# Banded attention and two MLPs: queries divided by the slope, and a part of VectorE's work given to GpSimd

## The chip, the cores and the metric

One core of one Trainium2 chip runs the whole program. The metric is the time of one execution on the device in microseconds (us). Less is better. TensorE is PE here, VectorE is DVE, ScalarE is ACT, GpSimd is POOL, and SyncE is SP, which issues the DMAs.

## The reference

```python
def _attn_ref(q, k, v, n_global, n_local):     # B 2, H 8, S 768, D 64; n_global 8, n_local 96
    scores = scale * np.matmul(q, k.transpose(0, 1, 3, 2))
    is_global = pos[None, :] < n_global
    is_local = (rel >= 0) & (rel < n_local)
    dist = np.where(is_global & ~is_local, n_local, np.abs(rel))
    slopes = 2.0 ** (-8.0 * (np.arange(H) + 1) / H)
    scores = np.where(is_global | is_local, scores - slopes[:, None, None] * dist, -1e9)
    a = np.exp(scores - np.max(scores, axis=-1, keepdims=True))
    a = a / (np.sum(a, axis=-1, keepdims=True) + 1e-09)
    return np.matmul(a, v)
def _moe_ref(x, w_in, w_out):                  # 1536 tokens, 512 -> 2048 -> 512
    h = np.maximum(x @ w_in, 0.0)
    return h * h @ w_out
def _moe2_ref(x, w_gate, w_val, w_out, rms_g): # 512 -> 1536 -> 512
    xn = x / np.sqrt(np.mean(x * x, axis=-1, keepdims=True) + 1e-06) * rms_g
    g = xn @ w_gate
    return (g / (1.0 + np.exp(-g)) * (xn @ w_val)) @ w_out
```

The output is `_moe2_ref(_moe_ref(attention))`, in float32.

## The kernel before, in words

**Three stages.** The attention comes first, in 16 slices (4 chunks of 384 tokens by 4 pairs of heads) of 3 tiles of 128 queries, so 48 tiles. The first MLP follows in 4 groups of hidden blocks; each group passes over the 4 token chunks, and the first passes of group 0 are mixed into the attention. Then the rows are normalised, and the second MLP is done with 7 products in place of 8 (sums of blocks are multiplied, lines 507 to 545).

**Products in three parts.** A float32 matrix is kept as a high part (fp32r, cast by ACT in L305) and a low part (the rest, a subtraction in L306). `mm3` issues three matmuls per product: high by high (L315), high by low (L316), low by high (L317). `xh`/`xl` are the split inputs of an MLP, `h` the hidden activations (L415 squares them), `M`, `ar` and `H` are slots for split weights, `b` is a bank of PSUM (the accumulators of the matmuls), `y` the sums of the first MLP (L446) and the output of the second (L588).

**Weights.** The weights come as eight-byte words and are turned into float32 by `expand()`: a DMA into `wraw` (L341), one ACT instruction (L344) and four of DVE on `wbits` (L345, L347, L349, L352). `block()` then splits the result. The low part (L306) is made on DVE for groups 0 and 1 and on POOL for the others.

**An attention tile.** The keys and queries of a slice arrive in `raw`. `prep` makes their high part `kqh` (L762 on ACT once, L764 on POOL) and low part `kql` (L766, DVE). PE multiplies them (L795, the "QK" product) into `ps`. L802 (DVE) adds the bias of the head and takes the row's extreme in one pass; the bias is a tile of its own for each head, made by POOL in L779 (`bw` for 256 keys, `bo` for 128). L806 (ACT) takes the exponential and the sum, L810 (DVE) adds 1e-9, L813 (DVE) takes the reciprocal, L815 (POOL) multiplies. PE transposes (`tb`, L822), ACT copies (`pt`, L824), PE multiplies by the values (`av`, L831).

**The norm.** `norm_sum` squares on ACT (into `nq`), adds three times on DVE (L464, `ns`), lets PE sum over the partitions with a matrix of ones (L466), takes the root on ACT (L469) and three reciprocals on DVE (L472). `norm(p)` then makes for each half of the tokens, twice, four scaled blocks (`fin`, L493, DVE) and four differences T1 to T4 (`diff`, L498, POOL), and splits all eight: the B blocks' low parts on DVE, the T blocks' on POOL (L306 with `ar<-nq` or `xl<-nq`).

**What sets the order.** Every instruction is put into a `Plan` with an engine, an assumed duration, the tiles it reads and writes, and for some a due time. `solve()` takes for each engine the ready instruction with the earliest due time, starts it when the assumed end of its predecessors plus a margin of their engine (`LAT`) is reached, and each engine's instructions are then written out in that order of starts. So a changed duration or margin can move any instruction, and on the chip an engine keeps its order whatever happens. Where PE has nothing planned before 30 us, `solve` puts in fillers, matmuls on a tile of zeros whose result nobody reads (L1085). At the end of the program a flag (L912 to L917) is loaded into a register of every engine (`values_load`, L1089) and a branch tests it (L1090); the branch holds a general attention that these inputs don't need.

## Time and profile before

| | before |
|---|---|
| runs, us | 705.15, 701.94, 702.2; median 702.2 |
| the profiled execution: its own time | 700.68 us |
| its span (first to last instruction) | 698.9 us |
| busy | PE 94%, DVE 71%, ACT 54%, POOL 36% |
| PE's clock over the span, of full speed | 0.997 |

The span is what the trace covers; 1.8 us of the execution's own time lie around it. "Busy" is an average over stages with different limits, so the rows below are cut by stretch: the attention (to about 165 us), the middle of the first MLP (to 330), its last group with the norms (330 to 470), and the second MLP (470 to the end).

### The profile page before, as it was taken

To read this page: it belongs to the slowest core of one execution; us is meant where nothing else is said; L and a number is where in the kernel's file an instruction comes from. 1 tells how busy PE (TensorE), PEld (TensorE's weight loads), DVE (VectorE), ACT (ScalarE), POOL (GpSimd) and SP (SyncE) were. 2 spreads that over 40 slices of the span, in tenths; PEclk is the share of its full clock that TensorE was granted. 3 is DMA by queue.
4 is the path that set the end of the run, shared out by engine and by line. 5 is a ranking of instruction groups with operands and counts; after the bars stand their busy time and mean duration, and the time that the engine had idled before them with its cause. 6 is when DMAs were issued, how large, how long until landed. Compare 5 with 4: busy or idle time off the path is not lost.

```text
span 698.9 us, 10714 instructions
## 1 busy us (share of the span) xinstructions
PE 657.8 (94%) x3876; PEld 591.8 (85%) x3876; DVE 495.2 (71%) x1025; ACT 374.4 (54%) x834; POOL 248.5 (36%) x298
## 2 busy tenths in 40 slices
PE   6999999998999999989899788999999999999996
PEld 6766777778989999989898677899898898997994
DVE  4899975556787722258898997976967868768434
ACT  2778786778755433356765666654344344343320
POOL 4855655430022000022518567635234323332000
PEclk9999999999999999999999999999999999999999
DMA  4554643201333300003220000121220311210022
GB/s 141 181 164 143 196 133 97 75 24 59 101 112 122 121 1 0 1 31 118 94 61 1 30 32 30 61 92 59 78 75 30 115 53 44 91 61 0 2 76 110
DMA packets 18159, 52.69 MB, mean 75 GB/s; under 512 B 2608, under 2 KB 3888, under 8 KB 18096
## 3 DMA queue, kind: packets, MB, share of 16 engines
q1 hardware_dynamic: 18096, 51.92, 22.6%
q8 instruction: 32, 0.52, 0.3%
q14 instruction: 31, 0.25, 0.1%
HBM read 48.76 MB, written 3.15 MB: 74 GB/s over the span
## 4 chain that ended last, share of the span: by engine, by line
PE 31%; DVE 16%; ACT 2%; issue 2%; POOL 2%; POOLq 0%; DVEq 0%
PE b L315 10%; PE b L317 10%; PE b L316 10%; DVE wbits L349 3%; DVE h L306 2%; DVE ra L564 1%; DVE wbits L345 1%; DVE wbits L347 1%; DVE ns L472 1%; DVE xl L306 1%; DVE h L415 1%; DVE wbits L352 1%; DVE y L588 1%; DVE nq L493 1%; POOL nq L498 1%
## 5 line engine op out<-in xcount | busy, mean ns | idle before, releaser
L306 POOL TENSOR_TENSOR M<-wbits,M 128x512 fp32r<-128x512 f32 x60 | 82.0, 1371 | 254.3 <-ACT M L305 168.9
L315 PE MATMUL b<-xh,M 128*128 128x384 f32 x384 | 133.4, 347 | 1.2 <-DVE xl L306 1.2
L316 PE MATMUL b<-xl,M 128*128 128x384 f32 x384 | 129.1, 336 | 0.5 <-DVE xl L306 0.5
L317 PE MATMUL b<-xh,M 128*128 128x384 f32 x384 | 129.0, 336 | 0.0
L815 POOL TENSOR_SCALAR p<-p,rs 128x256 f32<-128x256 f32 (+1 forms) x96 | 59.2, 628 | 54.6 <-DVE rs L813 29.5
L315 PEld LDWEIGHTS b<-xh,M 128*128 128x128 f32 x384 | 72.2, 188 | 6.9 <-issue 1.9
L316 PEld LDWEIGHTS b<-xl,M 128*128 128x128 f32 x384 | 72.4, 189 | 2.7 <-DVE xl L306 1.0
L415 DVE TENSOR_TENSOR h<-ra,h 128x384 fp32r<-128x384 f32 x64 | 42.3, 666 | 42.9 <-ACT ra L414 42.7
L317 PEld LDWEIGHTS b<-xh,M 128*128 128x128 f32 x384 | 72.4, 188 | 0.1
L305 ACT CAST M<-wbits 128x512 fp32r<-128x512 f32 x68 | 41.9, 617 | 49.5 <-DVE wbits L352 27.1
L349 DVE SCALAR_TENSOR_TENSOR wbits<-wraw,wbits 128x512 int32<-128x512 int32 x68 | 62.3, 917 | 1.8
L588 DVE TENSOR_TENSOR y<-b,y 128x512 f32<-128x512 f32 x60 | 40.9, 688 | 28.2 <-PE b L317 27.9
L317 PE MATMUL b<-M,h 128*128 128x512 f32 x144 | 56.9, 395 | 3.9 <-DVE h L306 3.9
L315 PE MATMUL b<-M,h 128*128 128x512 f32 x144 | 56.9, 395 | 3.1 <-DVE y L588 3.0
L806 ACT ACTIVATE p<-p,mn 128x256 f32<-128x256 f32 (+1 forms) x96 | 46.5, 487 | 22.0 <-DVE mn L802 21.3
L412 ACT ACTIVATE ra<-b 128x384 f32<-128x384 f32 x64 | 31.1, 486 | 50.6 <-PE b L317 50.6
L316 PE MATMUL b<-M,h 128*128 128x512 f32 x144 | 56.8, 394 | 0.0
L344 ACT ACTIVATE wbits<-wraw 128x512 f32<-128x512 f32 x68 | 45.4, 668 | 18.1 <-DMA wraw<-in_w_gate_dram 7.5
L345 DVE TENSOR_SCALAR wbits<-wbits 128x512 f32<-128x512 f32 x68 | 39.3, 578 | 20.5 <-ACT wbits L344 18.6
L305 ACT CAST h<-ra 128x384 fp32r<-128x384 f32 x48 | 24.6, 514 | 46.4 <-DVE ra L564 45.7
L352 DVE SCALAR_TENSOR_TENSOR wbits<-wraw,wbits 128x512 int32<-128x512 int32 x68 | 48.2, 709 | 1.2
L316 PE MATMUL b<-h,ar 128*128 128x384 f32 x128 | 43.5, 339 | 3.4 <-DVE h L415 3.4
(125 smaller groups left out, 1613.9 us busy)
## 6 DMA issues: line engine op xcount, KB each, us to landing
wraw<-in_w_out_dram SPq DMA_DIRECT2D x28, 512.0 KB, 3.5
wraw<-in_w_in_dram SPq DMA_DIRECT2D x16, 512.0 KB, 3.5
wraw<-in_w_gate_dram SPq DMA_DIRECT2D x12, 512.0 KB, 3.4
wraw<-in_w_val_dram SPq DMA_DIRECT2D x12, 512.0 KB, 3.4
raw<-in_kq_dram SPq DMA_DIRECT2D x8, 480.0 KB, 4.0
v<-in_vab_dram SPq DMA_DIRECT2D x8, 384.0 KB, 3.1
out_dram<-y SPq DMA_DIRECT2D x12, 256.0 KB, 2.0
raw<-in_kq_dram SPq DMA_DIRECT2D x7, 416.0 KB, 3.3
```

Of the source, the lines that this page charges most:

```text
L305: self.op("ACT", ACT(n), lambda: nc.scalar.copy(dst()[0], src()), rs, [(x, "hi") for x in ws])
L306: self.op(eng, t(n), lambda: e.tensor_tensor(out=dst()[1], in0=src(), in1=f32(dst()[0]), op=ALU.subtract), rs + [(x, "hi") for x in ws], [ ...
L315: nc.tensor.matmul(ps, lhsT=wh, rhs=ah, start=first, stop=False, skip_group_check=True)
L316: nc.tensor.matmul(ps, lhsT=wh, rhs=al, start=False, stop=False, skip_group_check=True)
L317: nc.tensor.matmul(ps, lhsT=wl, rhs=ah, start=False, stop=last, skip_group_check=True)
L345: self.plan.add("DVE", FAST(512), lambda: v.tensor_scalar(out=tl(bits), in0=tl(bits), scalar1=LEAST, scalar2=MOST, op0=ALU.max, op1=ALU.mi ...
L349: self.plan.add("DVE", DVE(512), lambda: v.scalar_tensor_tensor(out=bi(), in0=tl(raw)[:, :, 0], scalar=29, in1=bi(), op0=ALU.logical_shift ...
L352: self.plan.add("DVE", DVE(512), lambda: v.scalar_tensor_tensor(out=bi(), in0=tl(raw)[:, :, 1], scalar=-(1 << 30), in1=bi(), op0=ALU.bitwi ...
L415: self.op("DVE", DVE(CH), lambda: nc.vector.tensor_tensor(out=get()[1], in0=t(), in1=f32(get()[0]), op=ALU.subtract), rt + hi, lo)
L588: self.op("DVE", DVE(DM), lambda tok=tok, ps=ps: nc.vector.tensor_tensor(out=self.o(tok), in0=ps(), in1=self.o(tok), op=ALU.add), [("b", b ...
L806: self.op("ACT", 0.33 + w / 1200, lambda j=j: nc.scalar.activation(tl(f"p{m}")[:, j, :w], tl(f"p{m}")[:, j, :w], AF.Exp, bias=tl(f"mn{m}") ...
L815: self.op("POOL", 0.2 + w / 800, lambda j=j: nc.gpsimd.tensor_scalar(out=tl(f"p{m}")[:, j, :w], in0=tl(f"p{m}")[:, j, :w], scalar1=rs()[:, ...
```

## The change

1. The queries are divided by the head's slope while they are split (high part on POOL, low part on DVE, both with a column of `inv`, eight POOL memsets). The distance tiles `rel` and `t0` then serve all heads, with the slope in the scale of the DVE pass; the sixteen bias tiles of L779 go.
2. The 1e-9 is added on POOL (L812) instead of DVE (L810).
3. The low parts of the weights of groups 0 and 1 are made on POOL, those of the T blocks of the norm on DVE.
4. The flag is computed and loaded inside the plan, with due times of 100 and 130 us; before, the load stood behind everything on every engine but SP.
5. The planner's margins are larger, its DMA cost is another, the ones-matmul gets a slack of 1 us, and fillers begin at 5 us and are 0.3 us apart.
6. The weights of group 3 go into other slots and are queued earlier (`in` behind group 1, `out` and the first gate weights behind group 2).

Numbers of lines in the changed kernel are mostly one higher (L306 is L307, L345 is L346); in the attention L795 is L797, L802 is L804, L813 is L815, L815 is L817.

```diff
-    def add(self, eng, dur, emit, r=(), w=(), due=None, mode=None, lat=None):
+    def add(self, eng, dur, emit, r=(), w=(), due=None, mode=None, lat=None, slack=0.0):
...
-                x = max(free[e], 1.0)
-                while x + 0.2 < t:
+                x = max(free[e] + 0.1, 5.0)
+                while x + 0.3 < t:
                     self.fill.append(x)
-                    x += 0.18
+                    x += 0.3
...
-                    heappush(wait[q.eng], (q.ready, q.n, q))
+                    heappush(wait[q.eng], (q.ready + q.slack, q.n, q))
...
-LAT = {"PE": 0.27, "DVE": 0.17, "ACT": 0.22, "POOL": 0.22, "SP": 2.2, "END": 0.0}
+LAT = {"PE": 0.35, "DVE": 0.28, "ACT": 0.33, "POOL": 0.4, "SP": 2.6, "END": 0.0}
...
-DMA = lambda kb: 0.3 + kb / 200.0
+DMA = lambda kb: max(0.45, kb / 320.0)
...
-            due=self.clock, mode="full")
+            due=self.clock, mode="full", slack=1.0)
...
-                self.split(tmp[n], get, CH, res[n], r, "POOL" if n[0] == "T" else "DVE")
+                self.split(tmp[n], get, CH, res[n], r, "DVE")
...
+                elif kind == "in":
+                    slot = self.ar_slot(G1 + f) if f else self.m_slot(8)
                 else:
-                    slot = self.m_slot((8, 0, 1, 2)[f]) if kind == "in" else self.ar_slot(G1 + 1 + f)
-                self.block((kind, g * G1 + f), slot, "DVE" if g < 2 else "POOL")
+                    slot = self.m_slot(f - 1) if f else self.ar_slot(8)
+                self.block((kind, g * G1 + f), slot, "POOL")
...
+            if g == 1:
+                self.weights("in", 3)
             if g == 2:
-                self.weights("in", 3)
                 self.weights("out", 3)
-        for kind in ("gate", "val", "out2"):
+                self.weights("gate", 0)
+        for kind in ("val", "out2"):
...
-            if s == 0 and n == 0:
+            if n == 1:
+                self.op("POOL", POOL1(w), lambda raw=raw, hi=hi: nc.gpsimd.tensor_scalar(
+                    out=hi(), in0=raw(), scalar1=inv(), scalar2=1.0, op0=ALU.mult, op1=ALU.mult), rr + ["inv"], rh)
+                self.op("DVE", DVE(w), lambda raw=raw, hi=hi, lo=lo: nc.vector.scalar_tensor_tensor(
+                    out=lo(), in0=raw(), scalar=inv(), in1=f32(hi()), op0=ALU.mult, op1=ALU.subtract), rr + rh + ["inv"], rl)
+                continue
+            if s == 0:
...
-            name = self.bias(2 * hp + j, i)
+            name = "rel" if i else "t0"
...
-        self.op("DVE", 0.2, lambda: nc.vector.tensor_scalar(
-            out=rs(), in0=tl(f"sm{m}"), scalar1=1.0e-9, scalar2=None, op0=ALU.add),
+        self.op("POOL", 0.15, lambda: nc.gpsimd.tensor_scalar(
+            out=rs(), in0=tl(f"sm{m}"), scalar1=1.0e-9, scalar2=1.0, op0=ALU.add, op1=ALU.mult),
...
+        plan.add("DVE", 1.0, lambda: said.update(flag=covered(nc, const, nl, ng)), ["nl"], ["flag"], due=100.0)
+        plan.add("SP", 1.0, lambda: said.update(value=nc.values_load(said["flag"][0:1, 0:1], min_val=0, max_val=1)),
+                 ["flag"], (), due=130.0)
...
-    flag = covered(nc, const, nl, ng)
-    value = nc.values_load(flag[0:1, 0:1], min_val=0, max_val=1)
-    with tc.If(value < 1):
+    with tc.If(said["value"] < 1):
```

**POOL, from the first bias to the first products of probabilities** (`p` holds probabilities, `rs` the reciprocal of their sums, `sm` the sums), before:

```order
L779 TENSOR_SCALAR bo_136<-t_130 128x128
L779 TENSOR_SCALAR bo_142<-t_130 128x128
L764 TENSOR_SCALAR kqh_125<-raw_85 128x384
L779 TENSOR_SCALAR bw_153<-rel 128x256
L779 TENSOR_SCALAR bw_159<-rel 128x256
L779 TENSOR_SCALAR bo_170<-t_130 128x128
L779 TENSOR_SCALAR bo_173<-t_130 128x128
L779 TENSOR_SCALAR bw_181<-rel 128x256
L764 TENSOR_SCALAR kqh_188<-raw_116 128x448
L764 TENSOR_SCALAR kqh_188<-raw_116 128x384
L779 TENSOR_SCALAR bw_208<-rel 128x256
L815 TENSOR_SCALAR p_177<-p_177,rs_205 128x128 x2
```

and now:

```order
L767 TENSOR_SCALAR kqh_129<-raw_83,inv 128x384
L775 TENSOR_SCALAR kqh_145<-raw_113 128x448
L767 TENSOR_SCALAR kqh_145<-raw_113,inv 128x384
L812 TENSOR_SCALAR rs_191<-sm_174 128x2
L817 TENSOR_SCALAR p_168<-p_168,rs_191 128x128 x2
L775 TENSOR_SCALAR kqh_129<-raw_83 128x448
L1079 TENSOR_LOAD flag
L812 TENSOR_SCALAR rs_238<-sm_200 128x2
L767 TENSOR_SCALAR kqh_129<-raw_83,inv 128x384
L817 TENSOR_SCALAR p_187<-p_187,rs_238 128x256 x2
```

The bias tiles are gone from between the splits, the adds and the load of the flag stand in the queue.

**PE, from its first instruction to the second QK product of the attention**, before and now:

```order
L1085 MATMUL b_93<-h_91 128x384 x30
L795 MATMUL ps_162<-kqh_125 128x128
L795 MATMUL ps_164<-kqh_125 128x128
L795 MATMUL ps_162<-kql_139,kqh_125 128x128
L795 MATMUL ps_164<-kql_139,kqh_125 128x128
L795 MATMUL ps_162<-kqh_125,kql_139 128x128
L795 MATMUL ps_164<-kqh_125,kql_139 128x128
L1085 MATMUL b_93<-h_91 128x384 x5
```

```order
L1096 MATMUL b_143<-h_81 128x384 x2
L797 MATMUL ps_151<-kqh_129 128x128
L797 MATMUL ps_153<-kqh_129 128x128
L797 MATMUL ps_151<-kql_138,kqh_129 128x128
L797 MATMUL ps_153<-kql_138,kqh_129 128x128
L797 MATMUL ps_151<-kqh_129,kql_138 128x128
L797 MATMUL ps_153<-kqh_129,kql_138 128x128
L1096 MATMUL b_143<-h_81 128x384 x5
```

Two fillers stand ahead of the first QK product in place of thirty; in all, 27 are left of 76.

**DVE, at the norm sum of the first chunk** (group 3 of the first MLP), before and now:

```order
L464 TENSOR_TENSOR ns_3266<-ns_3266,nq_3274 128x384
L446 TENSOR_TENSOR y_106<-b_620,y_106 128x384
L446 TENSOR_TENSOR y_106<-b_93,y_106 128x384
L345 TENSOR_SCALAR wbits_531<-wbits_531 128x512
L347 TENSOR_SCALAR wbits_531<-wbits_531 128x512
L464 TENSOR_TENSOR ns_3266<-ns_3266,nq_3306 128x384
L464 TENSOR_TENSOR ns_3266<-ns_3266,nq_3310 128x384
L349 SCALAR_TENSOR_TENSOR wbits_531<-wraw_254,wbits_531 128x512
```

```order
L465 TENSOR_TENSOR ns_3253<-ns_3253,nq_3267 128x384
L447 TENSOR_TENSOR y_121<-b_521,y_121 128x384
L447 TENSOR_TENSOR y_121<-b_143,y_121 128x384
L465 TENSOR_TENSOR ns_3253<-ns_3253,nq_3288 128x384
L465 TENSOR_TENSOR ns_3253<-ns_3253,nq_3293 128x384
L346 TENSOR_SCALAR wbits_260<-wbits_260 128x512
L348 TENSOR_SCALAR wbits_260<-wbits_260 128x512
L350 SCALAR_TENSOR_TENSOR wbits_260<-wraw_140,wbits_260 128x512
```

The two weight instructions have moved behind the norm's adds. Over the last five chunk passes of the first MLP, DVE has 24 of these weight instructions where it had 40; the other 16 now stand in the passes before 330 us.

## Rows read from the trace of the kernel before

**Rows 1.** Windows of the whole program: us; busy time (instructions) by engine; PE clock; DMA.
```profile
8.00:40.00 32.00, 30.53 (x240) 23.37 (x238) 24.22 (x93) 20.33 (x66) 25.81 (x49) 1.00 0.49 159
40.00:82.00 42.00, 40.44 (x305) 30.88 (x306) 40.23 (x119) 33.82 (x88) 21.34 (x29) 1.00 0.50 166
82.00:330.00 248.00, 241.96 (x1559) 221.69 (x1558) 146.94 (x359) 147.10 (x343) 56.60 (x82) 1.00 0.23 73
330.00:470.00 140.00, 125.29 (x662) 116.12 (x661) 122.60 (x173) 86.82 (x171) 80.63 (x69) 0.99 0.16 53
470.00:699.00 229.00, 217.02 (x1111) 197.18 (x1110) 157.25 (x266) 84.53 (x168) 62.55 (x59) 1.00 0.18 61
```

**Rows 2.** PE's waits in 330 to 470: engine line <- releaser: us, times, longest.
```profile
PE b L466 <- DVE ns L464: 5.4, 3, 2.2
PE b L317 <- DVE h L306: 3.9, 2, 3.3
...
PE b L316 <- DVE h L415: 1.2, 2, 0.7
```

**Rows 3.** Timeline of PE, 0 to 13: start, busy, instruction, idle before it.
```profile
5.47 6.88 PE L1085 MATMUL b<-h 128*128 128x384 f32 x30 [5.47 <-DVE h L1066]
12.28 0.33 PE L795 MATMUL ps<-kqh 64*128 64x128 f32 x2
```

**Rows 4.** Timeline of POOL, 0 to 13.
```profile
7.88 1.16 POOL L779 TENSOR_SCALAR bo<-t 128x128 f32<-128x128 f32 x2 [5.74 <-DVE t L869]
9.01 0.51 POOL L764 TENSOR_SCALAR kqh<-raw 128x384 fp32r<-128x384 f32 x1
```

**Rows 5.** Timeline of DVE, 0 to 13.
```profile
7.29 0.15 DVE L917 CAST flag<-cb 128x1 int32<-128x1 f32 x1
...
9.55 0.56 DVE L766 TENSOR_TENSOR kql<-raw,kqh 128x384 fp32r<-128x384 f32 x1 [1.03 <-POOL kqh L764]
```

**Rows 6.** Timeline of SP's DMA issues, 0 to 16.
```profile
10.18 0.33 SPq L737 DMA_DIRECT2D raw<-in_kq_dram  x1
```

**Rows 7.** DVE's groups by form, 8 to 82: busy us, mean ns, idle before.
```profile
L306 DVE TENSOR_TENSOR M<-wbits,M 128x512 fp32r<-128x512 f32 x8 | 6.5, 809 | 0.0
...
L810 DVE TENSOR_SCALAR rs<-sm 128x2 f32<-128x2 f32 x22 | 4.7, 215 | 0.2 <-ACT p L806 0.2
```

**Rows 8.** POOL's groups by form, 8 to 82.
```profile
L779 POOL TENSOR_SCALAR bw<-rel 128x256 f32<-128x256 f32 x8 | 3.6, 450 | 0.3
...
L779 POOL TENSOR_SCALAR bo<-t 128x128 f32<-128x128 f32 x8 | 2.8, 359 | 5.9 <-DVE t L869 5.7
```

**Rows 9.** POOL's groups by form, 330 to 470.
```profile
L306 POOL TENSOR_TENSOR M<-wbits,M 128x512 fp32r<-128x512 f32 x17 | 24.2, 1431 | 21.3 <-ACT M L305 16.4 <-issue 4.9
...
L306 POOL TENSOR_TENSOR ar<-nq,ar 128x384 fp32r<-128x384 f32 x12 | 15.4, 1294 | 0.9 <-ACT ar L305 0.9
...
L306 POOL TENSOR_TENSOR xl<-nq,xh 128x384 fp32r<-128x384 f32 x4 | 5.4, 1361 | 0.0
```

**Rows 10.** DVE's groups by form, 330 to 470.
```profile
L349 DVE SCALAR_TENSOR_TENSOR wbits<-wraw,wbits 128x512 int32<-128x512 int32 x14 | 15.0, 1073 | 0.3
...
L306 DVE TENSOR_TENSOR xl<-nq,xh 128x384 fp32r<-128x384 f32 x12 | 11.6, 964 | 1.9 <-ACT xh L305 1.8
```

**Rows 11.** Timeline of DVE around the first norm sum.
```profile
338.34 1.44 DVE L345 TENSOR_SCALAR wbits<-wbits 128x512 f32<-128x512 f32 x1 [1.64 <-POOL M L306]
339.81 0.43 DVE L347 TENSOR_SCALAR wbits<-wbits 128x512 int32<-128x512 int32 x1
340.16 1.22 DVE L464 TENSOR_TENSOR ns<-ns,nq 128x384 f32<-128x384 f32 x2
341.29 0.68 DVE L349 SCALAR_TENSOR_TENSOR wbits<-wraw,wbits 128x512 int32<-128x512 int32 x1
```

**Rows 12.** Windows around PE's longest stop in the second norm.
```profile
418.00:421.00 3.00, 0.00 (x0) 0.00 (x0) 3.00 (x3) 0.92 (x2) 3.00 (x4) 1.00 0.00 0
421.00:423.00 2.00, 1.37 (x4) 0.85 (x5) 2.00 (x4) 0.10 (x1) 0.98 (x1) 0.63 0.00 0
```

More of the change, by code (lines that the diff above doesn't have):

```diff
@@ L56 @@
 class Op:
-    __slots__ = ("eng", "dur", "lat", "emit", "deps", "succ", "due", "mode", "start", "end", "left", "ready", "n")
+    __slots__ = ("slack", "eng", "dur", "lat", "emit", "deps", "succ", "due", "mode", "start", "end", "left", "ready", "n")
 class Plan:
@@ L635, in rest @@
         self.weights("out", 2)
+        self.used = {}
+        self.ring = deque(self.m_slot(n) for n in (3, 4, 5, 6, 7, 8, 0, 1, 2))
         for g in range(1, N1):
@@ L711, in __init__ @@
                 tl.define(f"{k}{n}", pool, [P, 2], F32)
-        for h in range(H):
-            tl.define(f"bw{h}", pool, [P, W], F32)
-            tl.define(f"bo{h}", pool, [P, P], F32)
+        tl.define("inv", pool, [P, HP], F32)
         tl.define("rel", pool, [P, W], F32)
@@ L856, in iotas, with inverse @@
             nc.gpsimd.iota(kidx(), pattern=[[1, P]], base=0, channel_multiplier=0, allow_small_or_imprecise_dtypes=True)
-        self.op("POOL", 1.5, iotas, (), y1)
+        def inverse():
+            for h in range(H):
+                nc.gpsimd.memset(tl("inv")[h % 2 * D : h % 2 * D + D, h // 2 : h // 2 + 1], 1.0 / slope8(h))
+        self.op("POOL", 1.0, iotas, (), y1)
+        self.op("POOL", 0.8, inverse, (), ["inv"])
         ts = lambda o, i, s1, s2, p0, p1: lambda: v.tensor_scalar(
@@ L1065 @@
         att = Attention(nc, plan, tl, ap, psa, mlp, kq, vab, ident, nl, ng)
-        plan.add("DVE", 0.5, lambda: nc.vector.memset(f32(tl(f"h{HB - 1}")), 0.0), (), [("h", HB - 1)])
+        plan.add("DVE", 0.5, lambda: nc.vector.memset(f32(tl(f"h{HB - 1}")), 0.0), (), [("h", HB - 1)], due=4.5)
         plan.add("POOL", 1.5, lambda: (make_identity(nc, ident), nc.gpsimd.memset(ones, 1.0), nc.gpsimd.memset(epst, 1.0e-6)),
```

22 lines of the change are left out of this document (9 added, 13 removed).

## Prediction

> **What bounds the kernel now.** I first cut the span into stretches and read each engine's busy time [rows 1]. PE works nearly without a break from 82 to 330 us (241.96 of 248), so nothing that other engines save there can shorten it much. Three stretches are different. From 8 to 40 and from 40 to 82 PE lacks 1.47 and 1.56 us, 3.0 together, while DVE is full in the second of them (40.23 of 42) and POOL is the fullest of the helpers in the first (25.81 of 32). From 330 to 470, PE lacks 14.7 us (140 less 125.29), the largest loss of the program. In the second MLP it lacks 12.0 of 229.
>
> Then I read PE's waits in 330 to 470 [rows 2]: 5.4 us for the norm's adds on DVE (three waits, the longest 2.2), 3.9 us in two waits for a low part of `h` that DVE makes, 1.2 us for squared activations. Last I read the start. PE's first real product is issued at 12.28, right behind thirty fillers that took 6.88 us from 5.47 [rows 3], although its last input was there at 9.55 + 0.56 = 10.11 [rows 5]. That input was late too: DVE waited 1.03 us for POOL, which had made two bias tiles of 1.16 us first [rows 4, 5].
>
> **The change, part by part.** The sum is made against the profiled execution, 700.68 us, which is 1.5 below the median of the runs, 702.2.
>
> *Attention, to 163 us.* DVE loses its adds (22 by 215 ns, 4.7 us, in 8 to 82) and the weights' low parts (8, 6.5 us) [rows 7]: 11.2 us less. POOL loses the bias tiles (3.6 + 2.8 = 6.4 us [rows 8]) and gains 8 low parts of 1.43 us [rows 9], 11.4 us, and 22 small adds. No row shows such an add on POOL: below, DVE's 0.215 for the same is the nearest; above, POOL's 0.359 for 128 columns [rows 8]. I take the lower, as the operand has two columns: 4.7 us (up to 7.9). So POOL goes from 47.2 to 56.9 of 74 us [rows 1]. It doesn't become full on average.
>
> POOL's work slows DVE. Where it is busy 58% of the time, L349 takes 1073 ns in the mean [rows 10] against 0.68 us by itself [rows 11], 0.39 more; a single L345 took 1.44 where its like, L347, took 0.43 [rows 11], 1.0 more. I take between 0.39 and 1.0 for each low part that comes to POOL, 3.1 to 8 us, and 4 for the sum, nearer to the mean of fourteen than to the single case. The Trainium skill states the harder rule (SBUF — State Buffer, section "Who interferes with whom"): a DVE instruction with two SBUF inputs, or in a two-port mode, and a GpSimd instruction that reads SBUF exclude each other, and the loser is blocked for the whole instruction. By that rule the eight would cost up to 11.4 us, DVE would have 2.9 us more work than before with the load below, and the sum would end at 697.1; the rows agree that there is a loss, and their 0.39 is far from the whole 1.43.
>
> The flag's load now stands in the middle of five queues. Between the flag's cast, done at 7.44, and SP's next DMA at 10.18 lay 2.74 us [rows 5, 6]; but that DMA stood right behind the split that ended at 10.11 [rows 5], which may be what held it. So a load costs an engine 0 to 2.74. I take 2.7 once, on DVE, where it sits between the two L802 of one tile. DVE is left with 11.2 - 4 - 2.7 = 4.5 us less work. At the start, two fillers instead of thirty stand ahead of the first product; it should come about when its inputs are there, so near 9, 3 us earlier. But an earlier start is worth only what the queue behind it can use: PE lacks 3.0 us between 8 and 82, and DVE and POOL stay nearly as full. I take **1.5 us** gained, half of it. Bounds: 6 gained (3.0 and the 3 of the start), 5 lost (contention at 8, another load that stops a second engine for 2.74, and the adds at 7.9: 8 + 5.5 + 3.2 - 11.2 = 5.5).
>
> *82 to 330 us.* DVE takes over 16 weight instructions from the later passes, by 0.43 to 1.07 each [rows 10, 11], 7 to 17 us, into a stretch where it is busy 147 of 248 [rows 1]. Cost 0, since PE is what bounds there; if DVE's order put them ahead of squared activations, 2.
>
> *330 to 470 us.* Here the gain should be. (a) Ahead of the first norm sum, DVE did two weight instructions (1.44 + 0.43 us [rows 11]) before the two last adds, while PE waited; these now follow the adds. The wait of 2.2 [rows 2] should go. (b) POOL loses the T blocks' splits, 15.4 + 5.4 = 20.8 us [rows 9], and DVE gets them, 16 by 0.56 (a like subtraction [rows 5]) to 0.96 (L306 on DVE in this stretch [rows 10]): 9.0 to 15.4 us. DVE gives away the 16 weight instructions, 7 to 17. So its own load stays about level, and POOL, which slows it, has 20.8 of 80.6 us less. The stop of PE on the low part of `h` (3.9 us) came in a run of DVE instructions while POOL was busy without a break [rows 12]; I let it go, with the clock that it cost: 2 us at 0.63 of full speed just behind it [rows 12], 0.7. (c) The 1.2 us for squared activations, late for the same reason, go as well. Together 2.2 + 3.9 + 0.7 + 1.2 = **8.0 us**. What is late next is the second and third norm sum (3.2 us), which I leave, and the norm's own chain. Bounds: 14.7 + 0.7 = 15.4 gained; 2.2 alone, if (b) only changes who is late.
>
> *470 to the end.* The order there is the same but for slots. 0. At the end, four engines loaded the flag behind their last work and now don't. SP's last DMAs run beside that and hide it: 0, at best the 2.74 of a load.
>
> **The sum:** 700.68 - 1.5 - 8.0 = 691.2; 1.5 above it for the median: **692.7 us**.
>
> **The rivals.**
> - *POOL becomes the bound of the attention, and the kernel is slower.* POOL keeps its order, and an add of 1e-9 or a scaling of probabilities that stands behind a low part waits 1.43 us; now each tile's chain goes through POOL twice. For it: POOL was at 25.81 of 32 us in the first twelve tiles [rows 1]. Against it: the averages above, and that PE has matmuls of the MLP between. If each of the 16 low parts is paid in full, it costs 22.9 us. It decides from 13.0 on (9.5 gained, and 3.5 more), so if 57% is paid. Paid at 80%, 18.3 us: about 711.
> - *The clock.* After PE's stop at 418 to 421 the granted clock was 0.63 [rows 12], the lower level of 1.2 GHz in part of that window, against 2.4 GHz elsewhere. Before, fillers kept PE at work from 5.47, and it was at full speed from 8 on [rows 1]; now PE is idle up to the first product and has a third of the fillers. At the lower level for the first twelve tiles (to 40 us), with 30.5 us of work of which at least 6.9 is filler, PE would pay up to some 20 us; since it is then busy without a break, I expect it back sooner, and take 8. By the Trainium skill (TensorE: Matmul & The Clock Gate, section "Part 1: The HAM clock gate") the gate opens again by PE's own activity; the mean of 0.99 over 330 to 470 [rows 1], so a quick return, agrees. Then the change ends near 700.7.
> - *A new wait in the second norm.* DVE is full in 330 to 470 (122.6 of 140) and gets 9 to 15 us of splits of which PE's first products there need the T blocks at once. If this makes a stop of 8 us, only the start's gain is left: 700.7.
> - *More is gained.* If all of the 15.4 goes, 702.2 - 1.5 - 15.4 = 685.3.
>
> **How the numbers follow.** A measurement of this kernel tells about 0.5%, 3.5 us, from no change: faster is below 698.7, slower above 705.7. The forecast has 0.57, the larger gain 0.13, together 0.70 faster. The clock has 0.07 and the new wait 0.10, 0.17 the same. POOL as the bound has 0.13, slower. The range goes from 681 (the larger gain with 4 of the bounds of start and end) to 705 (both neutral cases, with 4 us of the attention's lower bound).
>
> **What would show it.** Right: the first L797 near 9; DVE less busy and POOL more in 8 to 82; from 330 to 470 PE lacking about 7 us instead of 14.7, no wait of 2 us at the first L467, and no stop of 3 us on `h` near 420. Wrong: PE waiting in the attention for `p` of L817 or `rs`, a granted clock well below 1.00 before 40 us, or a long wait for a T block's low part (DVE L307).

## The result and the profile after

The changed kernel takes 695.74 us (median of 4 runs, 694.71 to 697.24); the kernel before took 703.18 beside it (701.94 to 705.15). The ratio is 0.9893, with a 95% interval from 0.986 to 0.9926: 7.4 us, 1.1% faster. 692.7 was predicted, in a range from 681 to 705.

The traced execution of the changed kernel took 696.2 us of its own time, with a span of 694.3, so the two traces stand 4.5 us apart and the medians 7.4. Stages are compared between the traces, so they add up to 4.5. To compare them I took marks that are the same work in both: the start of the last QK product of the attention, and of the PE matmuls of the MLPs counted from the program's last one.

| start of, us | before | after | after less before |
|---|---|---|---|
| last QK product | 156.1 | 155.9 | -0.2 |
| the matmul 2,700 before the last | 154.6 | 156.9 | +2.3 |
| 1,900 before the last (middle of the first MLP) | 303.2 | 306.4 | +3.2 |
| 1,000 before the last (second MLP has begun) | 491.0 | 487.8 | -3.2 |
| the last | 692.4 | 688.0 | -4.4 |

So between these two traces the attention lost 2.3 us, 0.9 more went to the middle of the first MLP, the stage with the norms gained 6.4, and the second MLP 1.2. The attention's number is the least certain of these. Two kernels of the next section, u_tsplit and b_tsplit, have the same order of instructions as the changed kernel and the kernel before up to the norms, so their traces are second executions of the same attention. They pass the mark at 155.1 and 155.3. The changed attention is thus between 2.4 us slower and 0.2 us faster, depending on which executions are compared. The windows of the changed kernel (us; busy time of PE, its weight loads, DVE, ACT, POOL; PE's clock; DMA share and GB/s) say the same, to be read against [rows 1]:

```profile
8.00:40.00 32.00, 28.39 (x186) 20.48 (x186) 27.33 (x86) 20.28 (x63) 23.14 (x39) 1.00 0.51 170
40.00:82.00 42.00, 39.37 (x289) 29.80 (x287) 36.19 (x99) 31.39 (x88) 34.32 (x51) 0.92 0.47 146
82.00:330.00 248.00, 242.44 (x1572) 222.63 (x1572) 151.11 (x335) 151.20 (x347) 85.33 (x125) 1.00 0.25 79
330.00:470.00 140.00, 130.86 (x690) 121.33 (x690) 118.97 (x184) 86.43 (x171) 53.09 (x46) 0.99 0.14 46
470.00:699.00 229.00, 212.91 (x1093) 194.01 (x1091) 149.30 (x259) 83.87 (x165) 62.96 (x59) 0.99 0.17 58
```

From 40 to 82 us, where before DVE was full (40.23 of 42), it is now busy for only 36.19, yet PE has less done, and at a clock of 0.92; POOL went from 21.34 to 34.32. DVE's missing work did not help PE. From 330 to 470 PE lacks 9.1 us in place of 14.7. PE's waits in that stretch, total, times and longest:

```profile
PE b L317 <- DVE h L416: 2.1, 5, 0.7
PE b L316 <- DVE b L535: 1.8, 1, 1.8
PE b L316 <- DVE ra L565: 1.3, 1, 1.3
...
PE b L318 <- DVE h L307: 0.8, 1, 0.8
PE b L467 <- DVE ns L465: 0.3, 1, 0.3
```

Against [rows 2], the norm's adds (L465) hold PE for 0.3 us in place of 5.4, and the low part of `h` (DVE L307) for 0.8 in place of 3.9. Waits for results of the second MLP's products were 3.7 us before:

```profile
PE b L315 <- DVE ra L542: 2.5, 4, 1.0
PE b L315 <- ACT b L528: 1.2, 2, 1.1
```

They are 4.4 now (L535, L565, and 1.3 for L543).

### The profile page after: what moved, and what is told of

It reads as the page before. It is cut to its first block, busy times and chain, and to the rows that moved or that the text cites. A ratio compares the mean times of both kernels' runs of the same rounds, so it can differ in the third digit from the quotient of the medians.

```text
span 694.3 us, 10667 instructions
## 1 busy us (share of the span) xinstructions
PE 655.4 (94%) x3827; PEld 589.1 (85%) x3827; DVE 487.7 (70%) x978; ACT 375.0 (54%) x834; POOL 262.7 (38%) x338
## 4 chain that ended last, share of the span: by engine, by line
PE 68%; DVE 22%; ACT 4%; issue 2%; POOL 2%; DMA 0%; DVEq 0%; ACTq 0%; POOLq 0%
PE b L316 20%; PE b L317 19%; PE b L318 19%; PE ps L797 4%; PE av L833 3%; PE tb L824 3%; DVE wbits L350 3%; DVE wbits L348 3%; DVE h L416 2%; DVE wbits L346 2%; DVE wbits L353 2%; DVE xl L307 1%; DVE ra L565 1%; DVE h L307 1%; DVE nq L494 1%
## 5 line engine op out<-in xcount | busy, mean ns | idle before, releaser
L307 POOL TENSOR_TENSOR M<-wbits,M 128x512 fp32r<-128x512 f32 x68 | 94.1, 1385 | 207.9 <-ACT M L306 142.4
L316 PE MATMUL b<-xh,M 128*128 128x384 f32 x336 | 117.3, 349 | 2.5 <-DVE ra L565 1.3
L317 PE MATMUL b<-xl,M 128*128 128x384 f32 x336 | 114.2, 340 | 1.1 <-DVE xl L307 1.1
L318 PE MATMUL b<-xh,M 128*128 128x384 f32 x336 | 113.8, 339 | 0.5 <-POOL M L307 0.5
L316 PEld LDWEIGHTS b<-xh,M 128*128 128x128 f32 x336 | 63.9, 190 | 6.8 <-DVE ra L565 1.6
L416 DVE TENSOR_TENSOR h<-ra,h 128x384 fp32r<-128x384 f32 x64 | 43.7, 688 | 36.0 <-ACT ra L415 36.0
L317 PEld LDWEIGHTS b<-xl,M 128*128 128x128 f32 x336 | 64.0, 190 | 3.7 <-DVE xl L307 2.3
L817 POOL TENSOR_SCALAR p<-p,rs 128x256 f32<-128x256 f32 (+1 forms) x96 | 57.4, 610 | 21.7 <-DVE rs L815 20.3
L318 PEld LDWEIGHTS b<-xh,M 128*128 128x128 f32 x336 | 64.0, 190 | 0.8 <-POOL M L307 0.8
L306 ACT CAST M<-wbits 128x512 fp32r<-128x512 f32 x68 | 41.9, 617 | 40.2 <-DVE wbits L353 15.5
L317 PE MATMUL b<-h,M 128*128 128x384 f32 x176 | 59.8, 340 | 3.3 <-DVE h L416 3.3
L316 PE MATMUL b<-h,M 128*128 128x384 f32 x176 | 61.7, 350 | 0.3 <-ACT h L414 0.3
L345 ACT ACTIVATE wbits<-wraw 128x512 f32<-128x512 f32 x68 | 45.2, 666 | 26.1 <-DMA wraw<-in_w_gate_dram 10.9
L318 PE MATMUL b<-h,M 128*128 128x384 f32 x176 | 59.0, 335 | 0.0
L353 DVE SCALAR_TENSOR_TENSOR wbits<-wraw,wbits 128x512 int32<-128x512 int32 x68 | 53.5, 791 | 1.1
```

The source lines that it names most:

```text
L306: self.op("ACT", ACT(n), lambda: nc.scalar.copy(dst()[0], src()), rs, [(x, "hi") for x in ws])
L307: self.op(eng, t(n), lambda: e.tensor_tensor(out=dst()[1], in0=src(), in1=f32(dst()[0]), op=ALU.subtract), rs + [(x, "hi") for x in ws], [ ...
L316: nc.tensor.matmul(ps, lhsT=wh, rhs=ah, start=first, stop=False, skip_group_check=True)
L317: nc.tensor.matmul(ps, lhsT=wh, rhs=al, start=False, stop=False, skip_group_check=True)
L318: nc.tensor.matmul(ps, lhsT=wl, rhs=ah, start=False, stop=last, skip_group_check=True)
L345: self.plan.add("ACT", ACT(512), lambda: nc.scalar.activation(tl(bits), f32(tl(raw)[:, :, 1]), AF.Abs), rr, rb)
```

## The experiments

The kernel before ran beside each set of runs, with medians of 703.18, 702.15, 704.15 and 702.07. It moves by 2 us from set to set, so the table gives the ratio with its interval, and an effect below some 2 us is not settled by medians alone.

| kernel | median us | ratio to before | last QK | last matmul |
|---|---|---|---|---|
| changed | 695.74 | 0.9893 [0.986, 0.9926] | 155.9 | 688.0 |
| u_low | 690.08 | 0.9824 [0.9805, 0.9843] | 149.5 | 683.0 |
| u_fill | 693.22 | 0.9873 [0.9859, 0.9887] | 153.1 | 686.0 |
| u_flag | 694.31 | 0.9891 [0.9859, 0.9922] | 154.8 | 688.9 |
| u_tsplit | 699.12 | 0.9965 [0.9944, 0.9987] | 154.1 | 690.9 |
| m_low | 692.34 | 0.9828 [0.979, 0.9865] | 152.1 | 684.2 |
| c_lowfill | 688.95 | 0.9798 [0.9765, 0.9831] | 147.7 | 678.1 |
| u_slots | 696.51 | 0.9893 [0.9855, 0.9931] | 154.4 | 688.0 |
| u_margin | 698.88 | 0.9909 [0.9876, 0.9942] | 158.9 | 691.8 |
| c_lowfillflag | 687.29 | 0.9781 [0.9741, 0.9821] | 146.6 | 678.5 |
| c_low0fill | 689.07 | 0.9798 [0.9762, 0.9833] | 147.8 | 681.1 |
| c_lowfilladd | 690.85 | 0.9827 [0.9792, 0.9862] | 150.8 | 682.1 |
| b_tsplit | 699.36 | 0.9947 [0.9924, 0.9969] | 156.9 | 691.4 |

Last QK and last matmul are from each kernel's own trace, a single execution; with one order of instructions they can differ by some 2 us. The changed kernel, u_fill and m_low have the same order of instructions on PE, DVE and ACT (fillers apart), and on POOL too but for m_low's own instructions; so have u_low and c_lowfill. The other experiments move other instructions as well, because the planner makes a new order.

### What the attention lost: the low parts (u_low, m_low)

The stop that shows best is at 43 us. In the changed kernel's timelines (start, busy, instruction, idle before it), of DVE:

```profile
43.52 1.61 DVE L769 SCALAR_TENSOR_TENSOR kql<-raw,inv,kqh 128x384 fp32r<-128x384 f32 x1 [0.40 <-POOL kqh L767]
45.06 0.55 DVE L307 TENSOR_TENSOR xl<-av,xh 128x384 fp32r<-128x384 f32 x1
```

of POOL:

```profile
42.31 1.18 POOL L767 TENSOR_SCALAR kqh<-raw,inv 128x384 fp32r<-128x384 f32 x1
43.46 1.26 POOL L307 TENSOR_TENSOR M<-wbits,M 128x512 fp32r<-128x512 f32 x1
```

and of PE:

```profile
45.71 0.69 PE L833 MATMUL av<-pt,v 128*64 128x128 f32 x4 [2.14 <-issue]
```

L769 (the low part of a query, two inputs in SBUF) ran for 1.61 us beside POOL's low part of a weight (L307 at 43.46); at 33.48 in the same trace it took 0.83. The second trace of this order, u_tsplit's, has the same split at 1.61 us and the same stop of PE (2.15). Behind it in DVE's queue stood the split of `av`, done at 45.61, and PE wrote the next `av` at 45.71, after 2.14 idle ("issue" means that the profile shows no releaser; that it was this split is read from the times). In the window around it the granted clock fell:

```profile
40.00:50.00 10.00, 7.86 (x46) 5.75 (x45) 8.02 (x25) 5.00 (x14) 7.75 (x13) 0.76 0.57 178
```

**u_low** undoes the move of the low parts:

```diff
-                self.block((kind, g * G1 + f), slot, "POOL")
+                self.block((kind, g * G1 + f), slot, "DVE" if g < 2 else "POOL")
```

> The changed kernel with one part undone: the weights' low parts of groups 0 and 1 are made on DVE again (the plan reckons with it). Theory (POOL's low parts stretch and hold DVE in the attention, which loses about 3 us there up to its end): the last QK product and the first MLP passes come some 3 us earlier, at most as early as before the change, and the time falls from 695.7 to about 693. Rival (the attention's loss is the clock and the missing fillers): within 1 us of 695.7. Third (DVE was full from 40 to 82, so 13 us more work on it count in part): 699 or more.

690.08, 5.7 us below the changed kernel by medians and 4.9 by ratios: better than the theory had it, and the third view, on which the prediction's step for the attention rested, fell. The last QK product comes 6.4 us earlier though DVE has the low parts again. The same window of u_low has PE at work for 9.66 of 10 us, and full clock:

```profile
40.00:50.00 10.00, 9.66 (x80) 6.77 (x76) 9.33 (x27) 6.48 (x20) 7.86 (x14) 1.00 0.63 194
```

**m_low** keeps the changed kernel's plan and queues and takes away most of what POOL reads. It leaves out the low parts of groups 0 and 1 but for four columns:

```diff
...
+            def low():
+                nc.gpsimd.memset(f32(dst()[1]), 0.0)
+                nc.gpsimd.memset(f32(dst()[1]), 0.0)
+                nc.gpsimd.tensor_tensor(out=dst()[1][:, :4], in0=src()[:, :4], in1=f32(dst()[0])[:, :4], op=ALU.subtract)
+            self.op("ACT", ACT(512), lambda: nc.scalar.copy(dst()[0], src()), rb, [(x, "hi") for x in ws])
+            self.op("POOL", POOL2(512), low, rb + [(x, "hi") for x in ws], [(x, "lo") for x in ws])
...
```

> The changed kernel, its plan and its queues the same, but for the sixteen low parts of groups 0 and 1 POOL does two memsets of the whole tile and a subtraction on four of its columns: POOL is held for about as long, and reads almost nothing of SBUF. It leaves out these low parts but for four columns. Theory (POOL's reads stop DVE's instructions with two inputs): L769 and the weight instructions L350 and L353 in 8 to 163 us fall back to the durations of the kernel with low parts on DVE (about 720 and 780 ns in place of 910 and 943), and the last QK product comes at 150 to 152 as there, time 690 to 692. Rival (a low part holds POOL's queue, and the softmax chain behind it waits): nothing changes, last QK at 155 to 156, time 695 to 696. Third (DVE, freed of 13 us, is planned worse): as the rival, with no stop of PE on POOL's products.

692.34, ratio 0.9828. The groups by form from 8 to 163 us (busy us, mean ns, idle before), of DVE in the changed kernel:

```profile
L769 DVE SCALAR_TENSOR_TENSOR kql<-raw,inv,kqh 128x384 fp32r<-128x384 f32 x16 | 14.6, 910 | 2.0 <-POOL kqh L767 2.0
L353 DVE SCALAR_TENSOR_TENSOR wbits<-wraw,wbits 128x512 int32<-128x512 int32 x11 | 10.4, 943 | 0.1
```

in u_low:

```profile
L769 DVE SCALAR_TENSOR_TENSOR kql<-raw,inv,kqh 128x384 fp32r<-128x384 f32 x16 | 11.5, 720 | 1.6 <-POOL kqh L767 1.6
...
L353 DVE SCALAR_TENSOR_TENSOR wbits<-wraw,wbits 128x512 int32<-128x512 int32 x11 | 8.6, 782 | 0.2
```

and in m_low:

```profile
L779 DVE SCALAR_TENSOR_TENSOR kql<-raw,inv,kqh 128x384 fp32r<-128x384 f32 x16 | 11.7, 731 | 2.1 <-POOL kqh L777 2.1
...
L353 DVE SCALAR_TENSOR_TENSOR wbits<-wraw,wbits 128x512 int32<-128x512 int32 x11 | 8.2, 749 | 0.1
```

POOL in the changed kernel, and in m_low, where each low part has become two memsets (L364 is the like of L365) and the short subtraction:

```profile
L307 POOL TENSOR_TENSOR M<-wbits,M 128x512 fp32r<-128x512 f32 x8 | 11.1, 1388 | 0.2
```

```profile
L365 POOL MEMSET M<- 128x512 f32 x8 | 4.5, 566 | 0.5
...
L366 POOL TENSOR_TENSOR M<-wbits,M 128x4 fp32r<-128x4 f32 x8 | 2.1, 268 | 0.7
```

POOL is held for about 1.4 us per low part in both (two memsets of 0.57 and 0.53 and 0.27, against 1388 ns), and the queues are the same. Yet L769 falls from 910 to 731 ns and L353 from 943 to 749, to where they are with the low parts on DVE. The means hide that only a few instructions are long. Three of the sixteen L769, at 24.5, 43.5 and 75.0 us, take 1.62 us or a little more, each beside a low part on POOL; at the same places m_low has 0.62. The split at 43 us in m_low, and PE's stop behind it:

```profile
42.93 0.62 DVE L779 SCALAR_TENSOR_TENSOR kql<-raw,inv,kqh 128x384 fp32r<-128x384 f32 x1 [0.41 <-POOL kqh L777]
```

```profile
44.11 0.44 PE L843 MATMUL av<-pt,v 128*64 128x128 f32 x4 [0.83 <-issue]
```

Instruction by instruction, DVE's work between 8 and 82 us takes 5.5 us longer in the changed kernel than in m_low, 0.7 for each of the eight low parts there.

The time follows: the last matmul of PE comes 3.8 us earlier, of the 5.0 that u_low gains. With one order in both, one can also say where. PE's instructions in m_low are ahead of the changed kernel's by 0.3 us just before the stop at 43 us and by 4.4 at 52 us, after it and after the lower clock behind it; at the end it is 3.8. Against u_tsplit's trace, where the clock's fall behind the same stop is shorter, the lead there is 2.5. So most of the loss is that POOL's subtraction stretches DVE's instructions, and PE waits behind one of them; POOL's queue is not the cause. What makes up the other 1.2 us, the order that u_low changes or the memset's freedom to start at another moment, stays open. The Trainium skill's rule on the shared ports (SBUF — State Buffer, section "Who interferes with whom") excepts GpSimd instructions that only write from the contention with a DVE instruction of two SBUF inputs; the two memsets in m_low agree with that.

### The fillers (u_fill)

```diff
-                x = max(free[e] + 0.1, 5.0)
-                while x + 0.3 < t:
+                x = max(free[e], 1.0)
+                while x + 0.2 < t:
                     self.fill.append(x)
-                    x += 0.3
+                    x += 0.18
```

> The changed kernel with the old rule for fillers (from 1 us on, 0.18 apart). Theory: within 1 us of 695.7, because the lower clock at 40 to 50 us came behind a stop of PE of 2.1 us there, long after the last filler. Rival (clock): granted clock back to 1.00 before 82 us and 2 to 3 us less, about 693.

693.22, 2.5 us below the changed kernel by medians and 1.4 by ratios; the last matmul 2.0 earlier. The intervals of the two ratios overlap, but the order of all other instructions is the same, so the traces can be compared one by one. The clock was the cause, in part where I did not look for it. The QK products of the changed kernel, from PE's timeline:

```profile
5.63 0.47 PE L797 MATMUL ps<-kqh 64*128 64x128 f32 x2 [2.90 <-ACT kqh L773]
...
9.82 1.97 PE L1096 MATMUL b<-h 128*128 128x384 f32 x5
11.71 0.58 PE L797 MATMUL ps<-kqh 64*128 64x256 f32 x2
...
14.22 0.58 PE L797 MATMUL ps<-kqh 64*128 64x256 f32 x2
...
19.24 0.58 PE L797 MATMUL ps<-kqh 64*128 64x256 f32 x2
...
21.84 0.39 PE L797 MATMUL ps<-kqh 64*128 64x256 f32 x2
```

and of u_fill:

```profile
8.97 0.33 PE L797 MATMUL ps<-kqh 64*128 64x128 f32 x2
...
9.59 1.84 PE L1096 MATMUL b<-h 128*128 128x384 f32 x9
11.36 0.39 PE L797 MATMUL ps<-kqh 64*128 64x256 f32 x2
...
13.50 0.39 PE L797 MATMUL ps<-kqh 64*128 64x256 f32 x2
```

With two fillers ahead of it, PE took 0.58 us for a pair of 256 columns up to 19.24, and 0.39 from 21.84 on; with the old fillers it took 0.39 from the start, and so the second tile comes at 11.36, before the changed kernel's 11.71, and the third at 13.50 against 14.22. The fillers (L1096) say the same: between the first two tiles five of them stand in the changed kernel's trace, mostly 0.32 us from start to start, and nine in u_fill's, mostly 0.17. That is nearly twice, as between the clock's two levels (1.2 and 2.4 GHz). PE had done only two fillers before it waited 2.9 and 3.1 us for the first product's inputs. The column of the granted clock doesn't show it; for the stretch from 9 to 16 us of the changed kernel it says 1.00 (last but two):

```profile
9.00:16.00 7.00, 6.80 (x28) 5.27 (x29) 4.39 (x20) 2.79 (x10) 1.73 (x4) 1.00 0.59 199
```

The trace's record of the clock begins only at 21.4 us in the changed kernel and at 7.3 in u_fill, just where the fillers become faster, and the column counts the time ahead of the first entry as 1.00. In the seven traces with the new rule the record begins between 14.9 and 24.6 us, in the seven with the old one between 6.7 and 10.3. So for the start the clock is read from the durations, and the experiment shows what restored them.

From tile to tile the lead of u_fill is 1.6 us at 42 us, 2.9 behind the stop at 43 us, and 2.1 from the norms on. The first part is the start. The second is the lower clock behind the stop, which u_fill has too (0.83 from 40 to 50 us) but for a shorter time: from 50 to 60 us its clock is 1.00, the changed kernel's 0.90. c_lowfill against u_low, again one order, gains 1.8 us by 42 us. So the missing fillers cost 1.6 to 1.8 us at the start, and the theory's stop at 43 us was not their doing.

### Low parts and fillers together, and the best version (c_lowfill, c_low0fill, c_lowfillflag)

c_lowfill undoes both edits above.

> The changed kernel with two parts undone: low parts of groups 0 and 1 on DVE, and the old rule for fillers. Theory (low parts cost about 5.7, missing fillers about 2.5 alone): if the two act at different places, 687.5; if the missing fillers only cost because PE stopped at 43 us behind a stretched split, 690 as without them. Rival (fillers stand in PE's way): 691 or more.

688.95, between the two numbers: 6.8 us below the changed kernel, where the two edits alone gave 5.7 and 2.5. By ratios, which allow for the drift between the sets, it is 6.7, and 4.9 and 1.4 alone: within the noise the effects add. c_low0fill leaves group 1's low parts on POOL (`"DVE" if g < 1 else "POOL"`).

> As with the low parts on DVE and the old fillers, but only group 0's low parts on DVE; group 1's stay on POOL as in the change. Theory (low parts on POOL hurt where DVE and PE are both full, up to 82 us, and not in the part that PE bounds): 689, within 1 us of that kernel. Rival (they hurt wherever DVE works beside them): half of the loss is back, 691 to 692.

689.07, the same as c_lowfill. Low parts on POOL hurt in the stretch where DVE and PE are both short of time (group 0's run from 24 to 75 us), and group 1's, behind 150 us, cost nothing that can be measured.

c_lowfillflag also puts the flag back at the end:

```diff
-        said = {}
-        plan.add("DVE", 1.0, lambda: said.update(flag=covered(nc, const, nl, ng)), ["nl"], ["flag"], due=100.0)
-        plan.add("SP", 1.0, lambda: said.update(value=nc.values_load(said["flag"][0:1, 0:1], min_val=0, max_val=1)),
-                 ["flag"], (), due=130.0)
...
+    flag = covered(nc, const, nl, ng)
+    value = nc.values_load(flag[0:1, 0:1], min_val=0, max_val=1)
+    with tc.If(value < 1):
```

> The changed kernel with three parts undone: low parts of groups 0 and 1 on DVE, the old fillers, the flag loaded at the end. Theory (the early loads stand where no engine is short of time): 689, within 1.5 us of the kernel with two parts undone. Rival (the loads hold PE or DVE in the first tiles): 686 to 687. Third (a load at the end lies on the path): 690 and more, a longer tail.

687.29, the lowest median of all that ran, 8.5 us below the changed kernel. Its windows:

```profile
8.00:40.00 32.00, 32.00 (x252) 24.02 (x250) 28.27 (x98) 23.66 (x74) 26.52 (x44) 1.00 0.56 176
40.00:82.00 42.00, 42.00 (x341) 33.07 (x340) 39.64 (x116) 34.68 (x97) 32.48 (x50) 1.00 0.56 181
```

PE is without a gap from 8 to 82 us (its fillers are counted as work). Against c_lowfill the 1.7 us are inside both intervals, so whether the flag's place matters is not settled by this pair.

### The flag alone (u_flag)

The diff is the one above, on the changed kernel.

> The changed kernel with the flag computed and loaded at the program's end again. Theory: no engine is short of time where the loads stand now, 695.7 within 1 us. Rival (a load stops its engine by up to 2.7 us in the first tiles, and PE waits): 693, with tiles 2 to 12 earlier. Third (the loads at the end cost time): 697 to 698, with a longer tail behind the last matmul.

694.31 (692.09 to 697.54), by ratio the same as the changed kernel, within some 3 us; the order of other instructions moves too. The trace of the changed kernel is more exact. The load on DVE, and the two instructions on either side of it (L804):

```profile
L1079 DVEq TENSOR_LOAD <-flag x1: 545/545/545, 15.3 to 15.3; - x1
```

```profile
15.27 0.42 DVE L804 CUSTOM_DVE_ANT_0 p<-ps,rel 128x256 f32<-128x256 f32 x1 [0.82 <-PE ps L797]
...
15.96 0.42 DVE L804 CUSTOM_DVE_ANT_0 p<-ps,rel 128x256 f32<-128x256 f32 x1 [0.26 <-issue]
```

The load takes 0.55 us on DVE and 0.46 to 0.49 on the others. The second L804 starts 0.69 us after the first, where the pair of the tile before (12.76 and 13.11) lies 0.35 apart: DVE loses 0.34 us. In the kernel before, SP's load takes 0.46 us and ends, with two short instructions behind it, at 8.24, so at most 0.8 of the 2.74 us from the flag to SP's next DMA were the load's.

### The 1e-9 (c_lowfilladd)

```diff
-        self.op("POOL", 0.15, lambda: nc.gpsimd.tensor_scalar(
-            out=rs(), in0=tl(f"sm{m}"), scalar1=1.0e-9, scalar2=1.0, op0=ALU.add, op1=ALU.mult),
+        self.op("DVE", 0.2, lambda: nc.vector.tensor_scalar(
+            out=rs(), in0=tl(f"sm{m}"), scalar1=1.0e-9, scalar2=None, op0=ALU.add),
```

> As with the low parts on DVE and the old fillers, and the 1e-9 added on DVE again. Theory (DVE is the fuller engine in the attention and 48 adds of 0.2 us are 9.8 us less for it, of which PE gets a part): 691 to 693. Rival (the extra passage through POOL costs as much as the add): 689.

690.85, against 688.95: the move of the small add is worth about 1.9 us, and the last QK product shows 3.1. The intervals overlap and the order of the whole attention changes with it, so the sign is likely and the size is not settled.

### The norms (u_tsplit, b_tsplit, u_slots)

u_tsplit and b_tsplit change the same line, one in the changed kernel and one in the kernel before:

```diff
-                self.split(tmp[n], get, CH, res[n], r, "DVE")
+                self.split(tmp[n], get, CH, res[n], r, "POOL" if n[0] == "T" else "DVE")
```

(u_tsplit; b_tsplit is the reverse, alone.)

> The changed kernel with the T blocks' low parts on POOL again. Theory (the norms gained because POOL's 20.8 us went): PE lacks 3 to 5 us more between 330 and 470, so 699 to 701. Rival (the norms gained by the weights moved out of the way alone): within 1 us of 695.7 and PE lacks about 9 us there as now.

> The kernel before with one part of the change alone: the T blocks' low parts on DVE. Theory (this move gave most of the norms' gain by itself): 3 to 5 us less than before, 698 to 700, and PE lacks about 10 us between 330 and 470 in place of 14.7. Rival (it helps only with the weights out of DVE's way): within 1 us of before, because DVE is full there. Third: slower, DVE becoming late for the first products of the second MLP.

u_tsplit took 699.12, 3.4 us more by medians and 5.1 by ratios. b_tsplit took 699.36, 2.7 less than before. The two waits of u_tsplit's PE from 330 to 470 that matter:

```profile
PE b L318 <- DVE h L307: 3.3, 2, 3.0
PE b L317 <- DVE h L416: 2.4, 2, 2.2
```

and two of b_tsplit, with its window:

```profile
PE b L466 <- DVE ns L464: 5.5, 2, 3.3
...
PE b L317 <- DVE h L306: 1.1, 1, 1.1
```

```profile
330.00:470.00 140.00, 129.09 (x672) 120.78 (x671) 117.65 (x189) 85.55 (x171) 59.58 (x53) 0.96 0.17 53
```

With the T blocks on POOL, the 3-us stop on `h` is back (3.0 us in one piece); with this one line changed in the old kernel, that wait falls from 3.9 to 1.1 while the norm sum's waits stay (5.5, before 5.4). PE there lacks 10.9 us, before 14.7; the window's clock of 0.96 is lower than before. The line has an effect by itself, but a small one: by the marks 1,900 and 1,000 before the last the stretch takes 187.9 us before, 186.1 with this line alone (b_tsplit), 186.1 with everything but this line (u_tsplit), and 181.4 with both. So the line and the rest of the change give 1.7 and 1.8 us alone and 6.5 together. In b_tsplit the norm sums still wait, one of them longer than before (3.3).

u_slots puts group 3's weights back in place and time:

```diff
-                elif kind == "in":
-                    slot = self.ar_slot(G1 + f) if f else self.m_slot(8)
                 else:
-                    slot = self.m_slot(f - 1) if f else self.ar_slot(8)
+                    slot = self.m_slot((8, 0, 1, 2)[f]) if kind == "in" else self.ar_slot(G1 + 1 + f)
...
-            if g == 1:
-                self.weights("in", 3)
             if g == 2:
+                self.weights("in", 3)
                 self.weights("out", 3)
-                self.weights("gate", 0)
-        for kind in ("val", "out2"):
...
+        for kind in ("gate", "val", "out2"):
```

> The changed kernel with group 3's weights in their old slots and queued as before. Theory (most of the norms' gain, 4.7 of some 6 us, is the T blocks' splits): PE loses 1 to 2 us more between 330 and 470, time 697. Rival (the moved weights gave the gain): the wait of 2 us at the first ones-matmul is back with other waits of 3 us and more, time 700 or more.

696.51, ratio 0.9893, no different from the changed kernel. Its DVE around the first norm sum:

```profile
339.46 1.00 DVE L346 TENSOR_SCALAR wbits<-wbits 128x512 f32<-128x512 f32 x1
340.49 0.43 DVE L348 TENSOR_SCALAR wbits<-wbits 128x512 int32<-128x512 int32 x1
340.83 1.21 DVE L465 TENSOR_TENSOR ns<-ns,nq 128x384 f32<-128x384 f32 x2
```

and its PE:

```profile
342.77 0.34 PE L318 MATMUL b<-xh,M 128*128 128x384 f32 x1
342.94 0.81 PE L467 MATMUL b<-ns,ones 128*128 128x384 f32 x2
```

The weight instructions stand ahead of the two adds again, as in [rows 11], yet PE does not wait: the sum is done at 342.04 and the ones-matmul starts at 342.94, straight behind other products. In the old order it stood 1,718 matmuls from the end of PE's work; in u_slots it stands 1,712, in the changed kernel 1,715. These one or two products of three matmuls are not what saves the wait. Six matmuls 0.17 us apart are 1.0 us, less than the 2.2 of the wait; and u_slots' sum is done just when PE would have reached the old place.

What differs is DVE. Both times it has finished two sums of `y` when PE is at the same matmul (at 336.70 before, at 339.54 in u_slots). From there to the norm sum it takes 4.68 us before and 2.50 in u_slots. Of the 2.18 between them, 1.64 is the idle time ahead of L345 in the first line of [rows 11], in which DVE waits for POOL's low part of a weight, and 0.44 is that L345 itself, 1.44 us against 1.00. b_tsplit has the same 1.64 of idle time and the same wait of 2.2. Why POOL is not late there in u_slots, no experiment shows; the slots and the T blocks' line are not the reason.

### The margins (u_margin)

```diff
-LAT = {"PE": 0.35, "DVE": 0.28, "ACT": 0.33, "POOL": 0.4, "SP": 2.6, "END": 0.0}
+LAT = {"PE": 0.27, "DVE": 0.17, "ACT": 0.22, "POOL": 0.22, "SP": 2.2, "END": 0.0}
...
-DMA = lambda kb: max(0.45, kb / 320.0)
+DMA = lambda kb: 0.3 + kb / 200.0
```

> The changed kernel with the planner's old margins and DMA cost. Theory (wider margins keep an engine from waiting for a neighbour that is late, which matters where DVE is stretched): 697 to 699. Rival (margins only move instructions around): within 1 us of 695.7. Third (the wider margins delayed the attention's tiles): 693, with the last QK product 2 us earlier.

698.88, 3.1 us more by medians, 1.1 by ratios with intervals that overlap. In its trace, which is of its slowest execution, the last QK product is 3.0 later than the changed kernel's. The second MLP takes 201.4 us from the mark 1,000 before the end, as before (201.4), where the changed kernel takes 200.2. All ten other kernels with the new margins take 200.1 to 200.3 there, and b_tsplit with the old ones 201.4: the 1.2 us gained there are the margins'. For the rest, that they help is likely; how much isn't settled. The slack of the ones-matmul and the divided queries were not tried one by one, nor were two small parts of the change that its list leaves out: the masks are now planned ahead of the first splits, and the tile of zeros for the fillers has a due time.

## Why the prediction was right, and where it wasn't

**The sum.** 9.5 us were forecast, 7.4 came (0.0107 of the time). The sign and the place are right: the largest gain is from 330 to 490, and the middle of the first MLP and the second MLP hardly moved. That the size is near is in part luck. The sum was made against a trace of 700.68 us, quicker than any of the counted runs of that kernel (701.16 and more). Between the traces the stages add up to 4.4 (-2.3, -0.9, +6.4, +1.2), less than half of the 9.5; the other 3 us of the 7.4 can't be placed.

**330 to 470: right in cause for (b), near in size, half right in cause for (a).** 8.0 us were put there; the marks show 6.4 up to the one 1,000 before the end. Term (b), the T blocks' splits off POOL, is shown in both directions: taking it away costs 3.4 us, putting it alone into the old kernel gives 2.7, and in both the wait on the low part of `h` moves as the step said, 3.9 us to 1.1, and 3.3 to 0.8. Its size was given as 3.9 + 0.7; in the stretch itself it is worth 4.7 us with the rest of the change and 1.7 without. Term (a) named DVE's order as the cause of the 2.2 us at the first norm sum: two weight instructions, 1.44 + 0.43, ahead of the adds. The wait did go, but u_slots has the old order on DVE and no wait. The step left out the first number of [rows 11]: DVE had stood idle for 1.64 us ahead of these two, waiting for POOL. That idle time and the stretched L345 are the whole difference. Moving the two behind the adds is one way to be rid of it, POOL being in time is another. And not only the first of the three waits went but all (5.4 to 0.3). I had left 3.2 of that as "late next"; why they went is not shown. Term (c) went the other way: the waits for squared activations rose from 1.2 to 2.1, and those for the second MLP's results from 3.7 to 4.4. Terms over and under nearly cancel.

**The attention: the gain did not come.** +1.5 was taken; -2.3 came between the two traces and at best +0.2 between other executions, inside the bound of -5 given. The step that failed is the one from DVE's time to PE's. POOL's low parts were priced at 4 us of DVE's work, 0.5 for each of eight, and set against DVE's whole saving of 11.2 us. That price was not far off: 5.5 us by m_low. But undoing the move gains about 5 us of the program's time, although DVE then makes the low parts itself, so DVE's total was not what PE waited for. Shown instead: three of the queries' splits (L769) take 1.62 us in place of 0.62. Behind one of them PE stops for 2.1 us, and its clock falls (0.76 from 40 to 50 us).

The divided queries were taken as a saving alone (the bias tiles, 6.4 us of POOL), and their own price was left out. In 8 to 163 us, before:

```profile
L764 POOL TENSOR_SCALAR kqh<-raw 128x384 fp32r<-128x384 f32 x16 | 8.6, 536 | 0.0
```

```profile
L766 DVE TENSOR_TENSOR kql<-raw,kqh 128x384 fp32r<-128x384 f32 x16 | 9.0, 560 | 1.8 <-POOL kqh L764 1.8
```

and in the changed kernel:

```profile
L767 POOL TENSOR_SCALAR kqh<-raw,inv 128x384 fp32r<-128x384 f32 x15 | 13.0, 863 | 0.6
```

The high parts take 4.4 us more on POOL. The low parts on DVE (L769) take 720 ns even in u_low, 2.5 us more in all than L766.

By the Trainium skill's rule of exclusive ports (SBUF — State Buffer, section "Who interferes with whom") the sum was put at 697.1, with the attention 2.9 worse; the measured -2.3 is near to that, but not by the same path. That sum had 11.4 us of stretched work on DVE and 2.7 of a load, and the runs show 5.5 and 0.3.

**The clock** was given 0.07 and 8 us, and its place was right: the first products run at the lower rate up to about 21 us. The sign that was to show it, a granted clock well below 1.00 before 40 us, stayed hidden, because the column shows no clock ahead of the record's first entry. Its size was too large, 1.6 to 1.8 us were measured, and the forecast counted nothing of it: the start that was worked out as 3 us earlier became a second tile at 11.71 in place of 13.84, and the lead was gone by tile 12.

**POOL's queue** as the bound, the rival on the slower side, did not come. m_low, with the queue as it is and POOL held as long, is 3.4 us faster by medians and 4.6 by ratios.

**The flag** was priced at 2.7 on the first tiles. The trace shows 0.34 us lost on DVE, so that term should have been 0.3. The weights moved into the middle of the first MLP cost nothing that u_slots could show, as taken.

## What to carry to other kernels

Moving work off a full engine to an idle one pays only if the idle engine's work does not slow the full one: compare the duration of the neighbour with and without it, and then ask what stands behind that neighbour in its queue. In two stages of this kernel the subtraction was better on DVE, though DVE was the fuller engine there; in the middle of the first MLP, where PE sets the pace, its place made no difference. So such a choice is made by stage. A mean duration is a poor price for it, since a few instructions can carry all of the loss. When dummy matmuls are taken out of a start, look at the durations of the first real products, and not only at the clock's column.
